# 128-row one-hot transposes and a re-ordered start in a routed-attention and MLP kernel

## Chip, cores, metric

One core of one Trainium2 chip. The metric is device time in microseconds (us) of one execution; the profile's "span" is some 1.9 us shorter than it. Engine names in the profile: PE is TensorE's matmuls, PEld its weight loads, DVE is VectorE, ACT ScalarE, POOL GpSimd, SP SyncE.

## The reference, cut to what matters

Four batches of eight heads, 768 rows of 64. A query attends only to keys whose nearest centroid (of 16 per head) is the same; then an MLP with exact GELU.

```python
q_assign = np.argmax(np.einsum('bhsd,hcd->bhsc', q_n, c_n), axis=-1)
k_assign = np.argmax(np.einsum('bhsd,hcd->bhsc', k_n, c_n), axis=-1)
mask = q_assign[:, :, :, None] == k_assign[:, :, None, :]
scores = scale * np.matmul(q, k.transpose(0, 1, 3, 2))
scores = np.where(mask, scores, -1000000000.0)
attn = np.exp(scores - max); attn = attn / attn.sum          # ... shortened
h = attn_out @ w_in;  out = gelu(h) @ w_out
```

## The kernel before

Each head goes through the same stations. GpSimd splits q and k into two fp16 parts (`split`: value and remainder). TensorE transposes them (`tr_pe`, six 128x128 blocks for q, six for k) into a tile in PSUM, the memory that TensorE writes its results to in this kernel (its parts are called banks), and VectorE copies that to `T`. TensorE multiplies `T` with the centroids (`asn`); VectorE sums two halves, takes the maximum, and compares (`onehot`). TensorE transposes the one-hots (`one_pe`) and VectorE writes them as 16 extra rows of `T`, scaled, so that the score matmul itself adds the mask. Six score pairs (`scores`) and six exps on ScalarE follow, then the product with v (`av`), its normalisation on VectorE (`norm`) and, every second head, a transpose of the output (`fin`). Heads 1 to 9 do their transposes on TensorE, as here; later heads use DMA transposes.

```python
ps_sc = ctx.enter_context(tc.tile_pool(name="ps_sc", bufs=2, space=PSUM))   # scores: 2 x 2 banks
ps_a = ctx.enter_context(tc.tile_pool(name="ps_a", bufs=1, space=PSUM))     # assignments: 1 bank
ps_x = ctx.enter_context(tc.tile_pool(name="ps_x", bufs=1, space=PSUM))     # output product: 1 bank
ps_o = ctx.enter_context(tc.tile_pool(name="ps_o", bufs=2, space=PSUM))     # all transposes: 2 banks
...
def one_pe(i):
    oh = ohs[(i // 2) % NOH]          # [128, N, 2 heads, q/k, 32]
    e = i % 2
    t_ps = ps_o.tile([128, S], FP16, tag="op", name="oh_ps")
    for j in range(N):
        nc.tensor.transpose(t_ps[0:64, j * 128:(j + 1) * 128],
                            oh[:, j, e].rearrange("p b c -> p (b c)"), ident)
    nc.vector.tensor_scalar(Ts[i][D:D + C, 1, :], t_ps[32:32 + C, :], -1.0, None, op0=ALU.add)
    nc.vector.tensor_scalar(Ts[i][D:D + C, 0, :], t_ps[0:C, :], float(VAL), None, op0=ALU.mult)
...
# the order of issue: g(i, c) is just after score pair c of head i
elif h < PT:                                          # heads 2 to 9
    o = 4 if h == 2 else 0
    at(g(0, 4) if h == 2 else g(h - 2, 0), tr_pe, h, 0)          # q
    at(g(0, 5) if h == 2 else g(h - 2, 2), tr_pe, h, 1)          # k
    at(g(1, 1) if h == 2 else g(h - 2, 4), prep_asn, h, h > 2)   # asn q, asn k, onehot
    at(g(h - 1, 1 + o // 2) if h < 11 else g(10, 4), one_pe, h)
```

In the traces below each engine's instructions come in the order of issue. The four pools take 4 + 1 + 1 + 2 = 8 PSUM banks.

The softmax here doesn't subtract the row's maximum and nothing guards it: scores larger than these inputs give would overflow.

Of the kernel before, what the change touches and what calls it, by code (L numbers as in the profile page):

```python
# [9 lines left out]
FP16 = mybir.dt.float16  # L10
# [10 lines left out]
def kernel(  # L21
# [10 lines left out]
    nc = tc.nc  # L32
# [3 lines left out]
    B, H, S, D = q.shape  # L36
    HC, C, _ = centroids.shape
    DM, DF = moe_w_in.shape
    N = S // 128
    NH = B * H  # L40
    QB = S // 2
# [17 lines left out]
    ps_sc = ctx.enter_context(tc.tile_pool(name="ps_sc", bufs=2, space=PSUM))  # L59
    ps_a = ctx.enter_context(tc.tile_pool(name="ps_a", bufs=1, space=PSUM))  # L60
    ps_x = ctx.enter_context(tc.tile_pool(name="ps_x", bufs=1, space=PSUM))
    ps_o = ctx.enter_context(tc.tile_pool(name="ps_o", bufs=2, space=PSUM))
# [3 lines left out]
    def load(i, keng=None, veng=None):  # L66
# [4 lines left out]
        for name, src, eng in (("q", q, nc.sync), ("k", k, keng or nc.sync),  # L71
# [9 lines left out]
    q_raw, k_raw, v_raw = [raw_pool.tile([128, N, D], FP32, tag=n + "_raw", name=n + "_raw")  # L81
                           for n in "qkv"]
# [13 lines left out]
    def warm(n, cols=512):  # L96
        for _ in range(n):
            nc.tensor.matmul(w_ps[:, 0:cols], ones[:, 0:128], ones[:, 0:cols],  # L98
                             start=True, stop=True)
# [3 lines left out]
    ident = const.tile([128, 128], FP16)  # L103
# [17 lines left out]
    NOH = 3  # L121
    ohs = [const.tile([128, N, 2, 2, 32], FP16, name=f"oh{t}") for t in range(NOH)]
    for t in ohs:
        nc.vector.memset(t[:, :, :, :, 16:32], 0.0)

    sts, vraws = {}, {}

# [17 lines left out]
    Ts = {}  # L145

    def tr_pe(i, w, copy=None, pool=None):
        if i not in Ts:
            Ts[i] = t_pool.tile([128, 2, S], FP16, tag="T", name="T")
        st = sts[i]  # L150
        pl, tag = pool or (ps_o, "op")
        t_ps = pl.tile([128, S], FP16, tag=tag, name="tr_ps")
        for j in range(N):
            nc.tensor.transpose(t_ps[:, j * 128:(j + 1) * 128], st[:, w, j, :], ident)  # L154
        (copy or nc.vector.tensor_copy)(Ts[i][:, w, :], t_ps)  # L155
# [17 lines left out]
    q1_raw, k1_raw, v1_raw = raws.pop(1)  # L173
    sts[1] = st_pool.tile([128, 2, N, 2 * D], FP16, tag="st", name="st")
    vraws[1] = v1_raw
    nc.gpsimd.tensor_tensor(cent_norm, cent_ssq, half, op=ALU.pow)
    nc.vector.tensor_sub(sts[0][:, 1, :, D:2 * D], k_raw, sts[0][:, 1, :, 0:D])

    tr_pe(0, 0, copy=nc.scalar.copy, pool=(ps_sc, "sc"))
    warm(1, 256)  # L180
# [10 lines left out]
    def cent_tr():  # L191
        chl_ps = ps_a.tile([128, 2, 128], FP16, tag="asn", name="chl_ps")
        for w in range(2):
            nc.tensor.transpose(chl_ps[:, w], cent_hl[:, w].rearrange("p a d -> p (a d)"),
                                ident)
        nc.vector.tensor_copy(c_all, chl_ps)

    def tr(i):
        st = sts.pop(i)
        Ts[i] = t_pool.tile([128, 2, S], FP16, tag="T", name="T")  # L200
        nc.sync.dma_start_transpose(
            out=Ts[i].rearrange("c w (n p) -> c (w n) p", p=128),
            in_=st.rearrange("p w n c -> p (w n c)"))
# [5 lines left out]
    def asn(i, which, halves=True):  # L209
        h = i % H  # L210
        chs = slice(h * C, (h + 1) * C)
        if which == 0:
            asns[i] = ps_a.tile([128, 512], FP32, tag="asn", name="asn_ps")
        a_ps = asns[i][:, 0:2 * NA].rearrange("p (n w l c) -> p n w l c", n=N, w=2, l=2)
        t = Ts[i][:, which]
        for j in range(N):
            js = slice(j * 128, (j + 1) * 128)
            if halves:
                nc.tensor.matmul(a_ps[:, j, which], t[:, js], c_all[:, :, chs],  # L219
                                 start=True, stop=True)  # L220
            else:
                for e in range(2):
                    nc.tensor.matmul(a_ps[:, j, which, 0], t[:, js], c_all[:, e, chs],  # L223
                                     start=(e == 0), stop=(e == 1))
# [35 lines left out]
    def one_pe(i):  # L260
        oh = ohs[(i // 2) % NOH]
        e = i % 2
        t_ps = ps_o.tile([128, S], FP16, tag="op", name="oh_ps")
        for j in range(N):
            nc.tensor.transpose(t_ps[0:64, j * 128:(j + 1) * 128],  # L265
                                oh[:, j, e].rearrange("p b c -> p (b c)"), ident)
        nc.vector.tensor_scalar(Ts[i][D:D + C, 1, :], t_ps[32:32 + C, :],  # L267
                                -1.0, None, op0=ALU.add)
        nc.vector.tensor_scalar(Ts[i][D:D + C, 0, :], t_ps[0:C, :],  # L269
                                float(VAL), None, op0=ALU.mult)  # L270

    def aug(i):
# [9 lines left out]
    def one_first():  # L282
        half_ps = []
        for e in range(2):
            t_ps = ps_o.tile([128, S], FP16, tag="op", name="oh_ps")
            for j in range(N // 2):
                nc.tensor.transpose(t_ps[0:64, j * 128:(j + 1) * 128],
                                    ohs[0][:, e * (N // 2) + j, 0].rearrange("p b c -> p (b c)"),
                                    ident)
            half_ps.append(t_ps)  # L290
        one_q, one_k = half_ps
        T0 = Ts[0][D:D + C]
        nc.scalar.activation(T0[:, 0, QB:S], one_k[0:C, 0:QB], ACT_FN.Copy, bias=0.0,
                             scale=float(VAL))
        nc.vector.tensor_scalar(T0[:, 0, 0:QB], one_q[0:C, 0:QB],
                                float(VAL), None, op0=ALU.mult)
        for o, z in ((0, 128), (128, QB)):
            nc.vector.tensor_scalar(T0[:, 1, o:z], one_q[32:32 + C, o:z],
                                    -1.0, None, op0=ALU.add)
        tr_pe(1, 1, pool=(ps_x, "x"))  # L300
        nc.vector.tensor_scalar(T0[:, 1, QB:S], one_k[32:32 + C, 0:QB],
                                -1.0, None, op0=ALU.add)

# [118 lines left out]
        nc.gpsimd.dma_start(out=w_chunks[n][0], in_=w_chunks[n][1])  # L422


    tr_pe(0, 1, copy=nc.scalar.copy, pool=(ps_sc, "sc"))
    warm(1)
    nc.scalar.copy(sts[1][:, 1, :, 0:D], k1_raw)
    nc.gpsimd.tensor_sub(sts[1][:, 1, :, D:2 * D], k1_raw, sts[1][:, 1, :, 0:D])
    cent_tr()
    nc.vector.tensor_sub(sts[1][:, 0, :, D:2 * D], q1_raw, sts[1][:, 0, :, 0:D])  # L430
    warm(2)
    asn(0, 0, halves=False)
    asn(0, 1, halves=False)
    onehot(0, halves=False)
    warm(1)
    tr_pe(1, 0, copy=nc.scalar.copy, pool=(ps_sc, "sc"))
    one_first()
    split(2, vnow=False)
    load_w(0)
# [44 lines left out]
    def at(t, fn, *args, **kw):  # L484
        events.append((t, len(events), fn, args, kw))

    T, TS = [], {}
    t = 0.0
    for i in range(NH + 1):
        for c in range(N):  # L490
            if (i, c) in FC1:
                b = FC1[i, c]
# [26 lines left out]
    def g(i, c):  # L519
        return TS[i, c] + 0.01  # L520
# [20 lines left out]
    for h in range(1, NH):  # L541
        pair = h - h % 2
        if h == 1:
            at(g(0, 0), asn, h, 0, False)
            at(g(0, 1), asn, h, 1, False)
            at(g(0, 1), onehot, h, False)
            at(g(0, 3), one_pe, h)
        elif h < PT:
            o = 4 if h == 2 else 0
            at(g(0, 4) if h == 2 else g(h - 2, 0), tr_pe, h, 0)  # L550
            at(g(0, 5) if h == 2 else g(h - 2, 2), tr_pe, h, 1)
            at(g(1, 1) if h == 2 else g(h - 2, 4), prep_asn, h, h > 2)
            at(g(h - 1, 1 + o // 2) if h < 11 else g(10, 4), one_pe, h)
        else:
            if pair < 10:
                at(g(pair - 2, 3) if h % 2 else g(pair - 3, 5), prep_asn, h)
                to, tg = T[pair] - g(pair - 2, 5), T[pair] - g(pair - 1, 2)
            else:
                ta, to, tg = (17.5, 12.0, 5.0) if pair >= 12 else (12.5, 7.0, 3.0)
                t0 = T[pair] - ta + 4.0 * (h % 2)  # L560
                at(t0, asn, h, 0)
                at(t0 + 1.2, asn, h, 1)
                at(t0 + 1.21, onehot, h)
            if h % 2 == 1:
                at(T[pair] - to, ohtr, pair)
                at(T[pair] - tg, aug, pair)
# [46 lines left out]
```

## Time and profile before

302.98 us (302.97 to 303.14, 3 runs). From the profile's page, busy times and the chain of work that ended last, by engine:

```profile
PE 296.4 (98%) x3109; PEld 186.0 (62%) x3109; DVE 121.7 (40%) x284; ACT 216.0 (72%) x274; POOL 106.8 (35%) x182
...
PE 97%; ACT 1%; DVE 1%; issue 0%; DVEq 0%
```

Both lines say TensorE. They are averages over stages, and one stage matters here: the attention of heads 0 to 9, before the first MLP.

| stretch of the trace | what the chain (where said, the timeline) shows |
|---|---|
| 0 to 9.35 us | loading, splitting, centroid chain, head 0's one-hot; first scores at 9.35 |
| 9.35 to 14.0 us | two exps (1.52 us), then head 1's one-hots on TensorE and VectorE; timeline: head 0's six exps back to back on ScalarE (4.48 us) |
| 14 to 47.6 us | TensorE in nearly every piece; 4.85 us a head |
| 47.6 to 55.5 us | two exps (1.63 us), then mostly TensorE; timeline: ScalarE's exps back to back (11 in 8.30 us) |
| from 55.5 us | MLP and later heads, TensorE |

The chain of one head in the third stretch (start, duration, what; x6 counts the instructions of a group):

```profile
25.29 0.45 PE oh_ps L265 x6
25.74 0.43 PE sc_ps L311 x2
26.17 0.18 PE x_ps L326 x6
26.35 0.33 PE tr_ps L154 x6
...
27.38 0.44 PE fin_ps L350 x6
...
28.33 0.29 PE asn_ps L219 x12
```

The one-hot group takes 0.45 us where the other six transposes (`tr_ps`) take 0.33.

The same head on VectorE in order of time (start, duration, engine, line, what; in brackets the idle time before it and what ended it):

```profile
23.61 0.56 DVE L232 TENSOR_REDUCE asum<-asn_ps 128x192 f32<-128x384 f32 x1 [0.41 <-PE asn_ps L219]
24.20 0.36 DVE L239 TENSOR_REDUCE asn_ps<-asum 128x12 f32<-128x192 f32 x1
24.59 0.35 DVE L240 TENSOR_TENSOR oh_167<-asum,asn_ps 128x192 f16<-128x192 f32 x1
24.87 0.19 DVE L336 RECIPROCAL rec<-x_ps 128x6 f32<-128x6 f32 x1
25.09 0.56 DVE L337 TENSOR_TENSOR x_tok<-x_ps,rec 128x384 f16<-128x384 f32 x1
25.56 0.55 DVE L155 COPY T<-tr_ps 128x768 f16<-128x768 f16 x1
26.14 0.55 DVE L267 TENSOR_SCALAR T<-oh_ps 16x768 f16<-16x768 f16 x1
26.71 0.55 DVE L269 TENSOR_SCALAR T<-oh_ps 16x768 f16<-16x768 f16 x1
27.29 0.56 DVE L155 COPY T<-tr_ps 128x768 f16<-128x768 f16 x1
27.86 0.56 DVE L352 COPY xt<-fin_ps 128x768 f16<-128x768 f16 x1
28.66 0.56 DVE L232 TENSOR_REDUCE asum<-asn_ps 128x192 f32<-128x384 f32 x1 [0.24 <-PE asn_ps L219]
```

From 20 us on VectorE has one wait a head, 0.41 or 0.24 us, always for the assignment matmuls, and is otherwise at work without a gap above 0.05 us.

### The profile page before, as it was taken

Reading aid. Unit: us, or ns where it says so; the run is one execution under the profiler, and the core shown is the slowest. Engines: PE = TensorE matmul, PEld = TensorE weight load, DVE = VectorE, ACT = ScalarE, POOL = GpSimd, SP = SyncE. Lnnn points to the kernel's source line nnn. Section 1 sums busy time; section 2 is a strip of 40 time slices with the busy share of each in tenths; the row PEclk is TensorE's granted clock in tenths of the full one; section 3 lists DMA queues with packets and bytes.
Section 4 is the critical chain, followed back from the end, with each engine's and each line's share of the span. In section 5 each row is a group of like instructions: output and inputs, shape, how many; then the busy total and the mean of one; then the engine's idle time right before and its main releaser. Section 6 shows DMA issues by size and latency. Waiting matters only on the chain.

```text
span 301.1 us, 7413 instructions
## 1 busy us (share of the span) xinstructions
PE 296.4 (98%) x3109; PEld 186.0 (62%) x3109; DVE 121.7 (40%) x284; ACT 216.0 (72%) x274; POOL 106.8 (35%) x182
## 2 busy tenths in 40 slices
PE   8899999999999999999999999999999999999996
PEld 4577777666666666666566666666566665565444
DVE  5788987103564742122353742213344413000112
ACT  5889999956888888856788888855788883466000
POOL 3999999997034104572633104600000000000000
PEclk9999999999999999999999999999999999999999
DMA  6999999994369348966679436876032242100122
GB/s 219 341 297 274 264 263 202 240 197 131 63 176 218 81 99 224 199 187 157 134 175 185 119 82 209 165 97 131 2 89 53 71 52 46 38 0 0 44 97 70
DMA packets 74065, 42.85 MB, mean 142 GB/s; under 512 B 54320, under 2 KB 71088, under 8 KB 74032
## 3 DMA queue, kind: packets, MB, share of 16 engines
q1 hardware_dynamic: 69520, 38.09, 53.4%
q0 software_dynamic: 4224, 4.19, 8.3%
q8 instruction: 24, 0.39, 0.5%
q10 hardware_dynamic: 288, 0.10, 0.1%
q14 instruction: 9, 0.07, 0.1%
HBM read 27.30 MB, written 6.29 MB: 112 GB/s over the span
## 4 chain that ended last, share of the span: by engine, by line
PE 97%; ACT 1%; DVE 1%; issue 0%; DVEq 0%
PE hp L386 27%; PE op L412 24%; PE sc_ps L311 21%; PE x_ps L326 11%; PE op_alt L412 3%; PE asn_ps L219 3%; PE tr_ps L154 2%; PE w_ps L98 1%; PE oh_ps L265 1%; ACT p_sb L314 1%; PE fin_ps L350 1%; PE asn_ps L223 0%; PE hp_early L367 0%; DVE T L269 0%; DVE T L267 0%
## 5 line engine op out<-in xcount | busy, mean ns | idle before, releaser
L314 ACT ACTIVATE p_sb<-sc_ps 128x768 f16<-128x768 f32 x192 | 149.7, 810 | 21.3 <-PE sc_ps L311 12.8
L311 PE MATMUL sc_ps<-T 80*128 80x384 f16 x384 | 93.8, 325 | 0.6 <-ACT p_sb L314 0.4
L386 PE MATMUL hp<-xt,w_in_sb 128*128 128x384 f16 x504 | 85.0, 326 | 0.0
L326 PEld LDWEIGHTS <-p_sb 128*128 128x128 f16 x1152 | 54.7, 97 | 30.8
L386 PEld LDWEIGHTS <-w_in_sb 128*128 128x128 f16 x504 | 47.9, 98 | 30.4
L132 POOL CAST st<-q_raw 128x384 f16<-128x384 f32 x30 | 15.4, 513 | 78.9 <-DMA q_raw<-in_q_dram 57.3
L416 DVE COPY o_sb<-op 128x512 f32<-128x512 f32 (+1 forms) x22 | 14.8, 672 | 55.0 <-PE op L412 54.9
L232 DVE TENSOR_REDUCE asum<-asn_ps 128x192 f32<-128x384 f32 x29 | 16.2, 558 | 50.8 <-PE asn_ps L219 50.7
L311 PEld LDWEIGHTS <-T 80*128 80x128 f16 x384 | 26.2, 97 | 5.8 <-issue 0.9
L133 POOL TENSOR_TENSOR st<-q_raw,st 128x384 f16<-128x384 f32 x30 | 27.3, 911 | 2.4
L135 POOL TENSOR_TENSOR st<-k_raw,st 128x384 f16<-128x384 f32 x30 | 27.4, 912 | 2.4
L336 DVE RECIPROCAL rec<-x_ps 128x6 f32<-128x6 f32 x32 | 6.2, 193 | 43.8 <-PE x_ps L326 43.8
L337 DVE TENSOR_TENSOR x_tok<-x_ps,rec 128x384 f16<-128x384 f32 x32 | 17.8, 558 | 1.1
L219 PEld LDWEIGHTS <-T 128*128 128x128 f16 x348 | 14.6, 96 | 4.4
L219 PE MATMUL asn_ps<-c_all,T 128*128 128x32 f16 x348 | 16.5, 177 | 0.0
L134 POOL CAST st<-k_raw 128x384 f16<-128x384 f32 x30 | 15.1, 505 | 0.0
L275 DVE TENSOR_SCALAR T<-ohT 16x768 f16<-16x768 f16 x22 | 7.9, 361 | 8.0 <-DMA ohT<-oh_166 3.6
L239 DVE TENSOR_REDUCE asn_ps<-asum 128x12 f32<-128x192 f32 x29 | 10.5, 361 | 1.0
L154 PE MATMUL tr_ps<-ident,st 128*128 128x128 f16 x120 | 10.6, 228 | 0.2 <-DVE T L269 0.2
L154 PEld LDWEIGHTS <-st 128*128 128x128 f16 x120 | 8.2, 101 | 2.9 <-DVE st L163 0.8
L155 DVE COPY T<-tr_ps 128x768 f16<-128x768 f16 x17 | 9.4, 554 | 0.6
L278 DVE TENSOR_SCALAR T<-ohT 16x768 f16<-16x768 f16 x22 | 8.6, 391 | 0.3
(308 smaller groups left out, 404.8 us busy)
## 6 DMA issues: line engine op xcount, KB each, us to landing
q_raw<-in_q_dram SPq DMA_DIRECT2D x32, 192.0 KB, 4.1
k_raw<-in_k_dram SPq DMA_DIRECT2D x32, 192.0 KB, 4.1
v_raw<-in_v_dram SPq DMA_DIRECT2D x32, 192.0 KB, 4.4
out_dram<-o_sb SPq DMA_DIRECT2D x23, 256.0 KB, 2.2
w_in_sb<-in_moe_w_in_dram POOLq DMA_DIRECT2D x4, 512.0 KB, 10.4
w_out_sb<-in_moe_w_out_dram POOLq DMA_DIRECT2D x4, 512.0 KB, 11.9
T<-st SPq DMA_TRANSPOSE x22, 4.9
xt<-x_tok SPq DMA_TRANSPOSE x11, 2.9
```

The costliest lines, as they stand in the source:

```text
L132: nc.gpsimd.tensor_copy(st[:, 0, :, 0:D], q_raw)
L133: nc.gpsimd.tensor_sub(st[:, 0, :, D:2 * D], q_raw, st[:, 0, :, 0:D])
L135: keng.tensor_sub(st[:, 1, :, D:2 * D], k_raw, st[:, 1, :, 0:D])
L154: nc.tensor.transpose(t_ps[:, j * 128:(j + 1) * 128], st[:, w, j, :], ident)
L219: nc.tensor.matmul(a_ps[:, j, which], t[:, js], c_all[:, :, chs], start=True, stop=True)
L232: nc.vector.tensor_reduce(out=asum, in_=a_ps.rearrange("p n w l c -> p n w c l"), axis=AX.X, op=ALU.add)
L311: nc.tensor.matmul(s_ps[:, t, 0:QB], Ts[i][0:D + C, 1, c * 128:(c + 1) * 128], Ts[i][0:D + C, 0, t * QB:(t + 1) * QB], start=True, stop=True)
L314: nc.scalar.activation(ps[i][:, c, :].rearrange("p (t q) -> p t q", t=2), s_ps[:, :, 0:QB], ACT_FN.Exp, bias=0.0, scale=float(scale))
L326: nc.tensor.matmul(x_ps[:, j], ps[i][:, ch, j * 128:(j + 1) * 128], va[:, ch, 0:D + 1], start=(ch == 0), stop=(ch == N - 1))
L337: nc.vector.tensor_tensor(xtoks[i - i % 2][:, :, i % 2, :], x_ps[:, :, 0:D], rec.to_broadcast([128, N, D]), op=ALU.mult)
L386: nc.tensor.matmul(hp[:, t, 0:QB], w_in_sb[:, m, f * 128:(f + 1) * 128], xts[b][:, m, t * QB:(t + 1) * QB], start=(m == 0), stop=(m == NM ...
L412: nc.tensor.matmul(op[:, 0:w], gs[b][f][:, js], w_out_sb[:, f, ms], start=(f == 0), stop=(f == NF - 1))
```

## The change

Its intent: one-hot transposes at the full 128 weight columns (both heads of a pair at once, half of it unused), and an earlier start: the remainder of head 0's keys goes from VectorE to GpSimd, head 0's transposed keys are copied in halves by two engines, the centroid chain comes sooner, head 1's steps are re-ordered around the one-hots, and head 2's first transposes come one slot sooner.

```diff
-        nc.vector.memset(t[:, :, :, :, 16:32], 0.0)
+        nc.vector.memset(t, 0.0)
...
-    nc.vector.tensor_sub(sts[0][:, 1, :, D:2 * D], k_raw, sts[0][:, 1, :, 0:D])
+    nc.gpsimd.tensor_sub(sts[0][:, 1, :, D:2 * D], k_raw, sts[0][:, 1, :, 0:D])
...
+    def tr_halves(i, w):       # three transposes each, copied by ScalarE and by VectorE
...
-            nc.tensor.transpose(t_ps[0:64, j * 128:(j + 1) * 128],
-                                oh[:, j, e].rearrange("p b c -> p (b c)"), ident)
-        nc.vector.tensor_scalar(Ts[i][D:D + C, 1, :], t_ps[32:32 + C, :],
+            nc.tensor.transpose(t_ps[:, j * 128:(j + 1) * 128],
+                                oh[:, j].rearrange("p a b c -> p (a b c)"), ident)
+        nc.vector.tensor_scalar(Ts[i][D:D + C, 1, :], t_ps[64 * e + 32:64 * e + 32 + C, :],
...                             # the same for q, and in head 0
-    tr_pe(0, 1, copy=nc.scalar.copy, pool=(ps_sc, "sc"))
     warm(1)
+    cent_tr()
+    tr_halves(0, 1)
...
-    cent_tr()
-    nc.vector.tensor_sub(sts[1][:, 0, :, D:2 * D], q1_raw, sts[1][:, 0, :, 0:D])
...                             # asn and onehot of head 0
-    tr_pe(1, 0, copy=nc.scalar.copy, pool=(ps_sc, "sc"))
+    nc.vector.tensor_sub(sts[1][:, 0, :, D:2 * D], q1_raw, sts[1][:, 0, :, 0:D])
...                             # inside one_first:
-        tr_pe(1, 1, pool=(ps_x, "x"))
+        tr_pe(1, 0, pool=(ps_x, "x"))
...                             # head 1 in the list of events
-            at(g(0, 0), asn, h, 0, False)
-            at(g(0, 1), asn, h, 1, False)
-            at(g(0, 1), onehot, h, False)
-            at(g(0, 3), one_pe, h)
+            at(g(0, 0), tr_pe, h, 1)
+            at(g(0, 1), asn, h, 0, False)
+            at(g(0, 2), asn, h, 1, False)
+            at(g(0, 2), onehot, h, False)
+            at(g(0, 4), one_pe, h)
...                             # heads 2 to 9
-            at(g(0, 4) if h == 2 else g(h - 2, 0), tr_pe, h, 0)
+            at(g(0, 3) if h == 2 else g(h - 2, 0), tr_pe, h, 0)
```

More of the change, by code (lines that the diff above doesn't have):

```diff
@@ L196, in cent_tr @@
         nc.vector.tensor_copy(c_all, chl_ps)
+    def tr_halves(i, w):
+        for e, (pl, tag, copy) in enumerate(((ps_sc, "sc", nc.scalar.copy),
+                                             (ps_o, "op", nc.vector.tensor_copy))):
+            t_ps = pl.tile([128, S], FP16, tag=tag, name="tr_ps")
+            for j in range(N // 2):
+                nc.tensor.transpose(t_ps[:, j * 128:(j + 1) * 128],
+                                    sts[i][:, w, e * (N // 2) + j, :], ident)
+            copy(Ts[i][:, w, e * QB:(e + 1) * QB], t_ps[:, 0:QB])
     def tr(i):
@@ L264, in one_pe @@
         for j in range(N):
-            nc.tensor.transpose(t_ps[0:64, j * 128:(j + 1) * 128],
-                                oh[:, j, e].rearrange("p b c -> p (b c)"), ident)
-        nc.vector.tensor_scalar(Ts[i][D:D + C, 1, :], t_ps[32:32 + C, :],
+            nc.tensor.transpose(t_ps[:, j * 128:(j + 1) * 128],
+                                oh[:, j].rearrange("p a b c -> p (a b c)"), ident)
+        nc.vector.tensor_scalar(Ts[i][D:D + C, 1, :], t_ps[64 * e + 32:64 * e + 32 + C, :],
                                 -1.0, None, op0=ALU.add)
-        nc.vector.tensor_scalar(Ts[i][D:D + C, 0, :], t_ps[0:C, :],
+        nc.vector.tensor_scalar(Ts[i][D:D + C, 0, :], t_ps[64 * e:64 * e + C, :],
                                 float(VAL), None, op0=ALU.mult)
@@ L286, in one_first @@
             for j in range(N // 2):
-                nc.tensor.transpose(t_ps[0:64, j * 128:(j + 1) * 128],
-                                    ohs[0][:, e * (N // 2) + j, 0].rearrange("p b c -> p (b c)"),
+                nc.tensor.transpose(t_ps[:, j * 128:(j + 1) * 128],
+                                    ohs[0][:, e * (N // 2) + j].rearrange("p a b c -> p (a b c)"),
                                     ident)
@@ L422, in load_w @@
         nc.gpsimd.dma_start(out=w_chunks[n][0], in_=w_chunks[n][1])
-    tr_pe(0, 1, copy=nc.scalar.copy, pool=(ps_sc, "sc"))
     warm(1)
+    cent_tr()
+    tr_halves(0, 1)
     nc.scalar.copy(sts[1][:, 1, :, 0:D], k1_raw)
     nc.gpsimd.tensor_sub(sts[1][:, 1, :, D:2 * D], k1_raw, sts[1][:, 1, :, 0:D])
-    cent_tr()
-    nc.vector.tensor_sub(sts[1][:, 0, :, D:2 * D], q1_raw, sts[1][:, 0, :, 0:D])
-    warm(2)
+    warm(1)
     asn(0, 0, halves=False)
@@ L434 @@
     onehot(0, halves=False)
-    warm(1)
-    tr_pe(1, 0, copy=nc.scalar.copy, pool=(ps_sc, "sc"))
+    nc.vector.tensor_sub(sts[1][:, 0, :, D:2 * D], q1_raw, sts[1][:, 0, :, 0:D])
+    warm(3)
     one_first()
```

## The prediction

> **What bounds the kernel now.** The page's busy shares: TensorE 98%, ScalarE 72%, VectorE 40%, GpSimd 35%; the chain that ended last is TensorE for 97%, at full clock. So there are two ways to gain: start the scores sooner, or take time off TensorE's queue. By the chain the first scores start at 9.35 us. Head 0 is then paced by ScalarE (six exps in 4.48 us, 0.75 each); from about 14 to 47.6 us TensorE paces (46 exps were done in 37.7 us, 0.82 apart); from 47.6 to 55.9 us ScalarE again (11 exps in 8.30 us). What follows is on TensorE and untouched by the change.
>
> **One-hot transposes (the larger part).** Heads 1 to 9 have a group of six with 64-column weights each, head 0 has one too. In the chain such a group takes 0.45 us, six 128-column transposes 0.34; the score pair right after it takes 0.43 us, other pairs 0.33. So the 64-column form costs about 0.21 us a head. The Trainium skill, "TensorE: Matmul & The Clock Gate", section on weight-path perf modes, says fast weight load is on only for 128 weights; "TensorEngine Tiling (Array Packing)", Key Properties, says that changing the tiling mode drains TensorE. Both fit, though no run shows the causes yet. Only groups in the TensorE-paced stretch count: heads 2 to 8, 7 x 0.21 = 1.5 us. Laying the chain's pieces with these cuts against exps 0.75 us apart and two score buffers gave an estimate of 1.5 us too. VectorE is busy 4.4 to 4.6 of 5 us there, and the period falls from 4.85 to about 4.65 us a head, so some is lost to its buffers: I count 1.35 us.
>
> **Start.** The key remainder leaves VectorE (0.56 us); on GpSimd it takes 0.91 us after the power (ends 4.65), so it ends near 5.55 against 4.88: worse. Bought back: the key copy, one ScalarE piece of 0.80 us ending near 6.75, becomes two halves side by side, ending near 6.65; the centroid transposes go first; so the assignment matmuls don't wait for keys and end near 7.15 instead of 7.40. Head 1's query remainder (0.56 us) now stands between the one-hot and its copies on VectorE, mostly behind the transposes, and gives back 0.1 us. First scores near 9.1: 0.2 to 0.25 us sooner.
>
> **Head 1.** One transpose group (0.34 us) moves from the idle wait before the scores into head 0's slots, where TensorE has slack (4.58 busy of 5). Its one-hot comes about 0.4 us later, but one VectorE copy goes ahead; its scores are ready (near 13.75) before ScalarE ends head 0 (near 14.1). Worth about 0; so are the larger memsets.
>
> **Sum.** 302.98 - 1.35 - 0.2 = 301.4 us, range 300.7 to 302.3. Faster by over 2%: 0.01; within 2%: 0.98; slower by over 2%: 0.01.
>
> **What would show each step.** One-hot groups in the chain at 0.34 us and the scores after them at 0.33; head periods near 4.65 us in 20 to 47 us; first scores at about 9.1 us; the first MLP stage (55.5 us before) about 1.5 us earlier, and the rest as long as before.
>
> **What would make it wrong.** The 0.10 us after a one-hot group belongs to something else, halving the gain; ScalarE or VectorE soaks it up (TensorE waits for exps or for a freed PSUM buffer); GpSimd's key remainder is slowed by VectorE beside it, or head 1's later one-hot opens a gap near 13 us: then 302.3 or more. If heads 1 and 9 count too: 300.9.

## The result, and the profile after

The changed kernel takes 303.1 us (302.97 to 303.27, 4 runs), the kernel before 303.0 (302.97 to 303.14, 4 runs). The ratio is 1.0003, 95% interval 0.9985 to 1.002: the same, where 1.6 us less had been expected. Here and below, a ratio is the mean time of one kernel's fast runs over that of the other's in the same rounds, so it is not quite the ratio of the medians quoted.

The page of the changed kernel, busy times and chain by engine:

```profile
PE 296.0 (98%) x3110; PEld 186.6 (62%) x3110; DVE 123.0 (41%) x285; ACT 214.1 (71%) x273; POOL 108.0 (36%) x183
...
PE 94%; DVE 2%; ACT 2%; DMA 1%; issue 0%
```

The chain of the same head (line numbers are 9 higher than before):

```profile
25.39 0.34 PE oh_ps L274 x6
25.72 0.42 PE sc_ps L320 x2
26.14 0.18 PE x_ps L335 x6
26.32 0.44 PE tr_ps L154 x6
...
27.45 0.47 PE fin_ps L359 x6
...
28.44 0.29 PE asn_ps L228 x12
```

The one-hot group did fall from 0.45 to 0.34 us, as predicted. But the next transpose group rose from 0.33 to 0.44, and `fin_ps` from 0.44 to 0.47: what TensorE saved it spent a microsecond later, waiting. The score pair after the one-hots hardly moved (0.42 against 0.43). VectorE tells what TensorE waited for (in brackets the idle time before an instruction and what ended it):

```profile
25.66 0.55 DVE L155 COPY T<-tr_ps 128x768 f16<-128x768 f16 x1
26.24 0.55 DVE L276 TENSOR_SCALAR T<-oh_ps 16x768 f16<-16x768 f16 x1
26.81 0.55 DVE L278 TENSOR_SCALAR T<-oh_ps 16x768 f16<-16x768 f16 x1
27.39 0.56 DVE L155 COPY T<-tr_ps 128x768 f16<-128x768 f16 x1
27.96 0.56 DVE L361 COPY xt<-fin_ps 128x768 f16<-128x768 f16 x1
28.77 0.56 DVE L241 TENSOR_REDUCE asum<-asn_ps 128x192 f32<-128x384 f32 x1 [0.24 <-PE asn_ps L228]
```

Each line lies 0.10 or 0.11 us behind its partner of before, and the idle time is the same 0.24: VectorE keeps its pace to the hundredth, only shifted. The first copy ends at 26.21, which frees one of the two PSUM buffers for transposes; TensorE's second transposes, which by the order of allocation take that buffer, start at 26.27 in its timeline. At 17.88 to 21.56 us the chain of the changed kernel itself runs on VectorE, through the one-hot copies, the sum and the comparison to that first copy, and from there to the second transposes (21.60, 0.49 us). From VectorE's reciprocals, head for head, the period is 4.86 us (24.97 to 44.41 over four heads) against 4.85 before (24.87 to 44.27).

The start did not come sooner either: first scores at 9.33 us against 9.35. And head 1's first scores came later, 14.20 against 14.01:

```profile
13.59 0.56 DVE L278 TENSOR_SCALAR T<-oh_ps 16x768 f16<-16x768 f16 x1
...
14.20 0.11 PEld L320 LDWEIGHTS <-T 80*128 80x128 f16 x2 [0.71 <-DVE T L278]
```

The weight load of those scores waits for VectorE's one-hot copy of head 1 and starts 0.05 us after it ends (14.15). The profile puts the matmul's own wait down to ScalarE, whose last exp of head 0 ends at 14.20 too; with two score buffers that matmul needs only an earlier exp. ScalarE had run out of scores by then (its first exp of head 1 shows 0.54 us of idle time before it, 0.18 before the change).

Theories put to the test ("paces" means: sets the time of one head). **V**: in the stretch of 17 to 47 us a loop paces: VectorE's instructions of a head in a row, and one trip through TensorE (transposes into the freed buffer, assignment matmuls) back to VectorE's next sum. A TensorE saving outside that trip becomes a wait. **T**: TensorE paces after all, and the 128-column form only moved its cost to the next group. **S**: ScalarE's exps pace. (GpSimd, busy 4.75 to 4.83 of 5 us there, is no further candidate: it works ahead at 4.12 us a head, 24.09 to 28.21, the profile shows no engine waiting for it in 18 to 45 us, and a_hi below gets to 4.655 us a head with its work untouched.) **L**, for the start: VectorE's centroid scaling is held up by GpSimd's key remainder.

### The profile page after: what moved, and what is told of

Same layout as the page of the kernel before. It is cut to its first block, busy times and chain, and to the rows that moved or that the text cites. A ratio compares the mean times of both kernels' runs of the same rounds, so it can differ in the third digit from the quotient of the medians.

```text
span 301.2 us, 7415 instructions
## 1 busy us (share of the span) xinstructions
PE 296.0 (98%) x3110; PEld 186.6 (62%) x3110; DVE 123.0 (41%) x285; ACT 214.1 (71%) x273; POOL 108.0 (36%) x183
## 4 chain that ended last, share of the span: by engine, by line
PE 94%; DVE 2%; ACT 2%; DMA 1%; issue 0%
PE hp L395 27%; PE op L421 24%; PE sc_ps L320 20%; PE x_ps L335 11%; PE op_alt L421 3%; PE asn_ps L228 3%; ACT p_sb L323 2%; PE tr_ps L154 2%; DMA q_raw<-in_q_dram 1%; PE oh_ps L274 1%; PE fin_ps L359 1%; PE asn_ps L232 0%; PE hp_early L376 0%; PE w_ps L98 0%; DVE asum L241 0%
## 5 line engine op out<-in xcount | busy, mean ns | idle before, releaser
L154 PE MATMUL tr_ps<-ident,st 128*128 128x128 f16 x114 | 9.8, 223 | 0.2
```

The costliest lines, as they stand in the source:

```text
L154: nc.tensor.transpose(t_ps[:, j * 128:(j + 1) * 128], st[:, w, j, :], ident)
```

## The experiments

All kernels gave correct results in the comparison, the two with a reduced assignment too. "Before" is the kernel before, run on the same chip in the same rounds.

| run | what | us | before | ratio (95%) |
|---|---|---|---|---|
| b_oh128 | before + 128-row one-hots | 302.89 | 303.00 | 0.9996 (0.9982 to 1.001) |
| a_hi | changed, VectorE's sum cut | 301.65 | 303.00 | 0.9954 (0.9941 to 0.9968) |
| b_hi | before, VectorE's sum cut | 302.24 | 303.00 | 0.9976 (0.9964 to 0.9989) |
| a_re | changed, one-hots later | 305.44 | 303.00 | 1.0078 (1.0065 to 1.0092) |
| a_split | changed, assignment split | 302.65 | 303.21 | 0.9984 (0.9972 to 0.9996) |
| b_split | before, assignment split | 302.74 | 303.21 | 0.9987 (0.9975 to 0.9999) |
| b128_split | before + 128-row + split | 302.28 | 303.21 | 0.9973 (0.9961 to 0.9985) |
| a_cact | changed, scaling on ScalarE | 303.11 | 303.21 | 0.9997 (0.9985 to 1.0008) |
| b128_psa | b128_split + other bank | 303.17 | 302.96 | 1.0004 (0.9992 to 1.0016) |
| b_psa | b_split + other bank | 303.28 | 302.96 | 1.0010 (0.9998 to 1.0022) |
| a_psa | a_split + other bank | 303.71 | 302.96 | 1.0030 (1.0016 to 1.0044) |
| a_kdve | changed, key remainder on VectorE | 303.06 | 302.96 | 1.0006 (0.9994 to 1.0018) |
| a_h1 | a_split, head 1 as before | 302.60 | 302.92 | 0.9989 (0.9977 to 1.0002) |
| b128_s2 | b128_split, first copy sooner | 303.45 | 302.92 | 1.0017 (1.0004 to 1.0031) |

### The one-hots alone: b_oh128

```diff
 # kernel before, with the change's edits to memset, one_pe and one_first only
```

> The kernel before with the 128-row one-hot transposes alone. Theory V (VectorE's loop paces the stretch 17 to 47 us: its 14 to 15 instructions a head back to back, plus one wait for the assignment matmuls): within 0.3 us of 303.0, one-hot groups at 0.34 us in the chain, the transposes and assignment groups after them longer by as much. My prediction's account (TensorE paces): 1.35 us faster, 301.6.

302.89 us, 0.1 below before, inside V's 0.3 and far from my 301.6. Its profiled execution took 605 us, with a granted clock of 0.979 (a slower state that some executions fall into), and is not used, so what V expected of its groups was not checked on it; b128_split below has the same one-hots in a fast one. So the miss is not a gain lost to the other parts of the change: the one-hots alone are worth next to nothing.

### Taking work off VectorE: a_hi and b_hi

A result wrong on purpose: heads 3 to 9 are assigned by the high half of the centroids alone, so that VectorE's sum of the two halves (0.56 us) goes, while TensorE issues as many matmuls as before (each with 16 moving columns, not 32).

```diff
-                for e in range(2):
+                ne = 1 if i in HI else 2           # HI = range(3, 10)
+                for e in range(ne):
                     nc.tensor.matmul(a_ps[:, j, which, 0], t[:, js], c_all[:, e, chs],
-                                     start=(e == 0), stop=(e == 1))
+                                     start=(e == 0), stop=(e == ne - 1))
...
-            ... prep_asn, h, h > 2)
+            ... prep_asn, h, h > 2 and h not in HI)
```

> The changed kernel, wrong result on purpose: heads 3 to 9 are assigned by the high half of the centroids alone, so VectorE loses the 0.56 us sum of each of 7 heads, while TensorE issues as many assignment matmuls as before. Theory V: VectorE's loop falls from 4.86 to about 4.3 us a head, ScalarE (4.5) or TensorE (4.5 to 4.65) paces next, so 1.5 to 2.5 us faster than 303.1. Rival T (TensorE paces, the saving of the one-hots was given back on TensorE itself, for instance in the pair after them): within 0.3 us of 303.1. Rival S (ScalarE paces): within 0.3 us too.

> The same cut of VectorE's sum on the kernel before. Theory V: faster than 303.0, but by less than on the changed kernel, since the 64-column one-hots then cost TensorE 0.11 to 0.21 us a head for 7 heads: 0.8 to 1.5 us slower than a_hi. Rivals T and S: within 0.3 us of 303.0.

a_hi is 1.35 us below before on its chip, b_hi 0.76. T and S fall: no matmul and no exp was taken away, and the narrower assignment matmuls gave TensorE little (0.28 us in place of 0.29 for the twelve where neither waits). a_hi stays a little short of the 1.5 us that V named (against the changed kernel's 303.1 us of other rounds it is 1.45), and the two lie 0.6 us apart, less than the 0.8 named: a_hi has the changed start, and its head 1 began 0.45 us later than b_hi's (14.41 against 13.96). The chain of a_hi, then of b_hi, in the same head:

```profile
25.05 0.34 PE oh_ps L276 x6
25.39 0.42 PE sc_ps L322 x2
25.81 0.18 PE x_ps L337 x6
25.99 0.34 PE tr_ps L154 x6
...
27.02 0.34 PE fin_ps L361 x6
```

```profile
24.95 0.45 PE oh_ps L267 x6
25.40 0.43 PE sc_ps L313 x2
25.83 0.18 PE x_ps L328 x6
26.01 0.34 PE tr_ps L154 x6
...
27.04 0.34 PE fin_ps L352 x6
```

With VectorE's load cut, every group of six 128-column transposes takes 0.34 us, `fin_ps` too: the 0.44 and 0.47 of the two original kernels were 0.34 of work and a wait. Now TensorE paces (its transpose and assignment groups all take the shortest time that any run shows for them), and its own period can be read: 4.655 us a head in a_hi (24.07 to 42.69 over four heads), 4.785 in b_hi (23.96 to 43.10). That is the true worth of the wide form where TensorE paces: 0.13 us a head, 0.11 in the group and 0.02 in the pair after it. And the kernel before, at 4.85, was only 0.065 above TensorE's own 4.785: TensorE looked like the pace-maker because it nearly was.

### Filling VectorE's wait by order: a_re

```diff
-            at(g(h - 1, 1 + o // 2) if h < 11 else g(10, 4), one_pe, h)
+            at(g(h - 1, 3 if h < 9 else 1), one_pe, h)
```

> The changed kernel with correct result; one line: the one-hot transposes of heads 3 to 8 come two slots later, behind the second transposes of the head after, so that VectorE has the two one-hot copies to do while it now waits for the assignment matmuls. No instruction is added or removed. Theory V: the wait of 0.41 and 0.24 us a head closes over 6 heads, 1.5 to 2 us faster than 303.1. Rivals T and S: within 0.3 us, or slower.

2.4 us slower than before: V's expectation failed. The period rose to 5.26 us (25.81 to 46.84). VectorE's timeline with the later one-hots:

```profile
27.38 0.56 DVE L155 COPY T<-tr_ps 128x768 f16<-128x768 f16 x1 [0.32 <-PE tr_ps L154]
28.40 0.55 DVE L276 TENSOR_SCALAR T<-oh_ps 16x768 f16<-16x768 f16 x1 [0.47 <-PE oh_ps L274]
```

VectorE now waits 0.79 us in this head, since the things it does next come from TensorE later, and TensorE in turn waits for the normalised output (its weight loads for the output product show 0.43 us of idle time before them). So the pace is not set by the sum of VectorE's work alone, but by how the two queues hand over to each other; my first form of V was too simple.

### Shortening the trip through TensorE: a_split, b_split, b128_split

The query half of the assignment matmuls comes one slot sooner; nothing is added.

```diff
-            at(g(1, 1) if h == 2 else g(h - 2, 4), prep_asn, h, h > 2)
+            if h == 2:
+                at(g(1, 1), prep_asn, h, False)
+            else:
+                at(g(h - 2, 3), asn, h, 0)
+                at(g(h - 2, 4), asn, h, 1)
+                at(g(h - 2, 4), onehot, h)
```

> The changed kernel, result correct; for heads 3 to 9 the query half of the assignment matmuls comes one slot sooner, so that only the key half (6 matmuls, about 0.18 us, not 12 in 0.36) stands between VectorE's last transpose copy and its next sum. No instruction is added. Theory V (a loop: VectorE's work of a head in a row, then one trip through TensorE's assignment matmuls): VectorE's wait of 0.41 us falls to about 0.25, the head period from 4.86 to about 4.7 us, 0.7 to 1.2 us faster than 303.1. If VectorE's or TensorE's plain throughput paces, and not the loop: within 0.3 us.

> The same on the kernel before (64-column one-hots). Theory V with the period that TensorE alone showed in b_hi (4.77 us a head, against 4.65 in a_hi): 0.3 to 0.8 us faster than 303.0, TensorE then pacing at about 4.77.

> The kernel before with the 128-row one-hots and the split assignment, with the start of before. Theory V: faster than b_split by 0.3 to 0.8 us (7 heads at 0.12 less what is left of the loop), and equal to or faster than a_split by up to 0.3, as head 1's scores come sooner in the order of before. If the one-hot width is worth nothing even where TensorE paces: equal to b_split.

Period 4.79 us in a_split (24.88 to 44.05), 4.81 in b_split (24.82 to 44.07), 4.79 in b128_split (24.53 to 43.69). VectorE's 0.24 us wait in the heads with an output transpose went, and the 0.41 in the other heads stayed, where half of it was expected to go: there TensorE arrives late at the key half, having waited for the freed buffer (0.49 us for the second transposes in the chain of a_split). a_split gained 0.56 us on before, less than the 0.7 named; b_split gained 0.47, as expected. b128_split gained 0.93: 0.46 more than b_split, inside the 0.3 to 0.8 named, and 0.37 more than a_split, a little over the 0.3 named. But the 0.46 came only in part as expected, from 0.12 us a head: the periods differ by 0.02, and of the lead in the profiled executions 0.29 was there at the second reciprocal already (24.53 against 24.82), 0.08 of it from loads that came sooner and 0.10 from head 1. To that extent the number was right by luck. **b128_split is the best correct version: 302.28 us, below the kernel before in the same rounds, and below the changed kernel's 303.1 of other rounds**, with one schedule edit and the 128-row form, without the new start.

### Another bank for the one-hots: b128_psa, b_psa, a_psa

```diff
-        t_ps = ps_o.tile([128, S], FP16, tag="op", name="oh_ps")
+        pl, tag = (ps_a, "asn") if 3 <= i <= 8 else (ps_o, "op")
+        t_ps = pl.tile([128, S], FP16, tag=tag, name="oh_ps")
```

> b128_split, result correct, with the one-hot transposes of heads 3 to 8 written to the PSUM bank of the assignments, which is free then, so that a head's second transpose group finds the other transpose buffer free. Theory V, sharpened (the loop runs VectorE's work, then its first transpose copy, which frees one of two PSUM buffers, then TensorE's second transposes up to the assignment matmuls, 4.66 us in heads without the output transpose): the second transposes wait no longer (0.34 us in place of 0.44 to 0.49), the period falls from 4.79 towards TensorE's own 4.65 us, 0.5 to 1.0 us faster than b128_split: 301.3 to 301.8. If the buffer is not on the loop: within 0.2 us of b128_split.

> The same with the 64-column one-hots. With the buffer out of the way TensorE paces, at about 4.77 us a head: 302.3 to 302.7. The difference to b128_psa is what the one-hot width is worth once TensorE paces: 0.7 to 1.1 us (0.12 us for heads 2 to 8, and 0.2 at head 1). Rival: the width is worth nothing, equal to b128_psa.

> The same two schedule edits on the changed kernel: as b128_psa in the stretch, but 0.2 to 0.5 us slower in all, for the start of the change and its order of head 1 (first scores of head 1 at 14.1 to 14.2 against 13.8).

By the ratios, all three came out slower than their partners without the bank edit: b_psa by 0.7 us, b128_psa by 0.9 (where 0.5 to 1.0 faster was expected), a_psa by 1.4. b_psa missed its 302.3 to 302.7, and a_psa lies 0.5 above b128_psa, at the edge of the 0.2 to 0.5 named. From the chain of b128_psa:

```profile
22.00 0.57 DVE T L270
22.56 0.05 issue
22.61 0.32 PE asn_ps L219 x6
...
26.27 0.34 PE tr_ps L154 x6
```

Half of the expectation held: the second transposes wait no longer (0.34 us), so it was the buffer that they had waited for. But the query half of the assignments now waits for the same bank until VectorE has copied the one-hots out (ends 22.56, matmuls from 22.61): the wait moved one group on, and grew. The period is 4.895 us (24.88 to 44.46). The two widths differ by 0.1 us here, not by 0.7 to 1.1: TensorE doesn't pace here either.

### First copy sooner: b128_s2

```diff
-            at(g(0, 4) if h == 2 else g(h - 2, 0), tr_pe, h, 0)
+            at(g(0, 4) if h == 2 else g(h - 2, 0) if h in (3, 9) else g(h - 3, 4) + 0.02, tr_pe, h, 0)
```

> b128_split, result correct, with the first transposes of heads 4 to 8 emitted two slots sooner, so that VectorE copies them (and frees their buffer) before the normalisation of the head and not behind it. Theory V (the buffer freed by the first copy starts TensorE's half of the loop): the second transposes wait no longer, the period falls from 4.79 by up to 0.13, 0.2 to 0.8 us faster than b128_split, 301.5 to 302.1. It may fail if the normalised output now comes too late for the next product (a wait before the output products of 0.2 us or more): then equal or slower.

0.5 us slower than before, and by the ratios 1.3 slower than b128_split, where 0.2 to 0.8 faster was expected. Again the named wait went (second transposes at 0.34 us), and again the time came back elsewhere: the transposes now stand before a score pair and ScalarE's exps enter the chain (0.82 us of one exp in each head). The expectation allowed for a failure by another route, a wait before the output products of 0.2 us or more: at 21.3 us that is there (0.54 us, 0.24 in b128_split at the same place), in the next head it is 0.17.

### The start: a_cact and a_kdve

a_cact scales the centroids on ScalarE, ahead of its first transpose copy; a_kdve puts the key remainder back on VectorE.

```diff
 # a_cact (the two VectorE steps before it move up with it)
-    nc.vector.tensor_scalar_mul(cent_hl[:, 0], cent_sb.unsqueeze(1).to_broadcast(...), cent_rnorm)
+    nc.scalar.mul(cent_hl[:, 0], cent_sb.unsqueeze(1).to_broadcast(...), cent_rnorm)
 # a_kdve
-    nc.gpsimd.tensor_sub(sts[0][:, 1, :, D:2 * D], k_raw, sts[0][:, 1, :, 0:D])
+    nc.vector.tensor_sub(sts[0][:, 1, :, D:2 * D], k_raw, sts[0][:, 1, :, 0:D])
```

> The changed kernel, result correct, with the centroid scaling moved from VectorE to ScalarE. Theory L (at the start, VectorE's scaling waits for GpSimd's key remainder beside it: 0.54 to 0.75 us in place of 0.29, ending 0.08 us after it, each time): the scaling takes 0.3 us and the first scores come 5.3 to 5.45 us after the centroid power starts, in place of 5.62 to 5.74, so 0.2 to 0.3 us faster than 303.1. Rival (the start is bound by the key remainder and its two copies alone): first scores and time unchanged.

> The changed kernel with the key remainder of head 0 back on VectorE, at its place before the centroid chain; all else as changed. Theory L: with nothing large on GpSimd beside it the centroid scaling takes 0.29 us again; it starts behind the remainder, so the first scores come 5.2 to 5.5 us after the centroid power starts, against 5.62 to 5.74, and 0.1 to 0.3 us faster than the changed kernel, if centroids land as early. Rival: the scaling stays at 0.54 to 0.82 us, so GpSimd's remainder was not its cause.

What L rests on, first in the changed kernel, then in the kernel before:

```profile
4.47 0.91 POOL L177 TENSOR_TENSOR st<-k_raw,st 128x384 f16<-128x384 f32 x1 [0.20 <-ACT st L172]
4.72 0.74 DVE L183 TENSOR_SCALAR cent_hl<-cent_sb,cent_rnorm 128x128 f16<-128x128 f32 x1
```

```profile
5.18 0.29 DVE L183 TENSOR_SCALAR cent_hl<-cent_sb,cent_rnorm 128x128 f16<-128x128 f32 x1
```

The same instruction takes 0.29 us before and 0.74 after, and ends (5.46) 0.08 us after GpSimd's subtraction (5.38). In a_hi, a_re, a_psa, a_split and a_h1, all with the changed start, it took 0.54, 0.54, 0.54, 0.82 and 0.84 us, and each time it ended 0.08 us after GpSimd's. a_kdve, with nothing large on GpSimd, has 0.29 again, and a_cact 0.40 on ScalarE. So the stall is real, 0.25 to 0.55 us, and GpSimd's instruction is its cause. The Trainium skill, "SBUF — State Buffer", section "Who interferes with whom", states the rule: VectorE in a mode with two ports and GpSimd take a shared pair of ports for a whole instruction, and the later one blocks. These numbers agree with it; that this instruction ran in such a mode is not in the trace.

But lifting the stall did not shorten the time. a_cact's first scores come 5.46 us after the centroid power starts, just outside the 5.3 to 5.45 named and below the 5.61 to 5.74 of the five kernels with the changed start as it is; its time is 303.11 us, 0.1 below before, where 0.2 to 0.3 had been named. In a_kdve they come 5.86 us after it, and the time is 303.06, 0.1 above before: a miss, the remainder on VectorE now stands ahead of the centroid chain itself. The times of arrival of the first loads blur this: the first VectorE instruction, which waits for q, started between 3.20 and 3.48 us from run to run, whatever the kernel. Measured from there, the first scores came after 5.93 to 6.09 us in the seven traces with the start of before and after 5.86 to 6.36 in the five with the changed start and order (before, b_hi, b_split, b128_split, b128_psa, b_psa, b128_s2; after, a_hi, a_re, a_split, a_psa). No start was shown to be faster.

Sorted by the arrival of the centroids, the traces say a little more. Where the centroid power started 0.17 to 0.24 us after that first VectorE instruction, the first scores came after 5.93 to 6.04 us with the start of before (b_hi, b_split, b128_split, b128_psa, b128_s2) and after 5.86 and 5.94 with the changed one (after, a_split). Where it started 0.61 to 0.65 us after, they came after 5.98 and 6.09 (b_psa, before) and after 6.22 to 6.36 (a_hi, a_re, a_psa). So in these traces the changed start gains next to nothing when the centroids come early, and loses 0.1 to 0.4 us when they come late. a_cact, a late one, has 6.08: with the stall lifted its first scores came 0.14 to 0.28 us sooner than theirs.

### Head 1's order: a_h1

```diff
 # a_split, with head 1's steps as in the kernel before:
+    tr_pe(1, 0, copy=nc.scalar.copy, pool=(ps_sc, "sc"))      # before head 0's one-hots
-            at(g(0, 0), tr_pe, h, 1)                           # and the events of before
 ...
```

> a_split with the start of the change (key remainder on GpSimd, key copy in halves, centroid transposes first) but head 1 in the order of before. If the order of head 1 is what costs: head 1's first scores come 4.55 to 4.6 us after head 0's, as in before, b_split and b128_split (4.57 to 4.67), not 4.85 to 4.87 as in every kernel with the change's order, and the time is 0.2 to 0.4 us below a_split, 302.25 to 302.5. If the start costs: equal to a_split, 302.65, with that gap still closed.

The gap between head 0's and head 1's first scores is 4.57 us, as with the old order; every kernel with the new order shows 4.86 or 4.87 (after, a_hi, a_re, a_split, a_cact, a_psa, a_kdve). So the new order costs 0.3 us there (a_h1 puts head 2's first transposes back as well, so the two are not told apart). The time, 302.60 us, is only 0.05 below a_split and misses the 302.25 to 302.5 named: in its trace the first scores came at 9.41 us against a_split's 9.25 (q arrived within 0.02 us of it), so there the old order gave back at the start half of what it gained at head 1, and what is left is below what these runs resolve.

## Why the prediction was wrong

- **Wrong step: "from about 14 to 47.6 us TensorE paces".** From it followed "Only groups in the TensorE-paced stretch count: heads 2 to 8, 7 x 0.21 = 1.5 us". The runs show a loop of VectorE and TensorE at 4.85 us a head in that stretch, with TensorE's own work at 4.785 (b_hi) and 4.655 (a_hi). Shortening TensorE from the one to the other left the period at 4.86; the 4.65 that I had named came only with VectorE's sum gone. The gain became waits. The largest is for a transpose buffer that VectorE frees (0.33 to 0.44 us in the next transposes; gone in b128_psa, where that buffer is free). Together they make up the whole difference: a_hi's 4.655, and in the changed kernel 0.10 more in `tr_ps` of each head, 0.13 more in `fin_ps` of every second head (0.47 against 0.34) and 0.08 more in `asn_ps` of the other heads (0.37 against 0.29) give 4.86.
- **How it came about.** I read the chain's TensorE pieces as work. Some held waits of 0.1 us: with matmul records of 219 ns and only 56 ns between starts (0.34 us for six), neighbouring records overlap and such a wait leaves no idle time in the page, which showed TensorE busy for 5.00 of 5 us. The Trainium skill, "Perfetto Trace Analysis", section "Per-instruction lifecycle: what the profiler-reported window actually captures", says that a matmul's end is estimated and not observed; such overlapping records fit that, though no run here shows the true ends. `fin_ps` at 0.44 us next to 0.33 for the same six transposes was the clue.
- **The size of the one-hots, 0.21 us a head, was 0.13** where TensorE paces. The group's 0.11 was right. The other 0.10, the pair after the group, was listed under "what would make it wrong" and did belong to something else: the pair takes 0.41 to 0.42 us with the 128-column form too, so a drain on the way back to 128 columns is at most some 0.02 us of it. What the rest is stays open.
- **"Some is lost to its buffers: I count 1.35 us"**, 0.15 taken off 1.5, named the right suspect and gave it a tenth of its weight.
- **The start, 0.2 us: not reached.** The predicted GpSimd time of 0.91 us was right, and it "is slowed by VectorE beside it" was named as a risk; it was the reverse, VectorE held up by GpSimd, 0.25 to 0.55 us of the centroid chain. That this is where the gain went is in part argued: in the traces with late centroids a_cact's first scores came 0.14 to 0.28 us sooner than with the stall, but its time did not come down, and the loads' arrival varies by 0.3 us.
- **Head 1, "Worth about 0", cost 0.3 us** (4.87 against 4.57 between first scores). Its one-hot came 0.8 us later (12.34 against 11.55), not 0.4, and its last copy ended at 14.15, not near 13.75. In the kernel before, head 1's wide one-hots were worth 0.1 us (4.67 to 4.57).
- **Right:** the direction of each single piece on TensorE, and that little of the time lies outside the stretch: the rest of the kernel, from the first MLP on, took as long as before (from the table load for the first GELU to the end, 55.97 to 301.2 us against 55.91 to 301.1).

## What to carry to other kernels

Before costing a saving on the engine that the chain names, look at the second engine of the stretch in order of time, not by its busy share: if it runs without a gap but for one wait that comes back each round, suspect a loop of the two and test it by taking work off the second one. If it is a loop, the saving is worth only what the first engine's own work exceeds the loop by (here nothing: 4.785 us of work in a loop of 4.85). Two groups of the same instructions with different durations in the chain (0.33 and 0.44 us) mean that one of them holds a wait. And of four re-orderings here one gained (the split), two took away the wait that they aimed at and lost more at the next hand-over (the other bank, the sooner copy), and one made the wait longer (a_re): in this kernel cutting work (a_hi, 1.35 us, though with a wrong assignment) was surer than moving it.

## What the Trainium skill lacked or had wrong

- "TensorEngine Tiling (Array Packing)", Key Properties: it says that a change of tiling mode drains TensorE, with no cost. Here the step from 64-column weights back to 128 cost no more than 0.02 us a group (pair after it 0.43 against 0.41 to 0.42 us). That this step is a change of mode is my reading of the profile's 128\*64 beside the 128\*128 of the neighbours; a cost on the way in would be within the group's 0.11 us.
- "TensorE: Matmul & The Clock Gate", the section on weight-path perf modes: it gives about 2x for fast weight load. That agrees: the weight loads' records here show 110 ns for 64 columns and 97 for 128, 1.72 against 0.76 ns a column; a group of six transposes takes 0.45 against 0.34 us. The formula of the same page's section on LDWEIGHTS, columns over 1.2, gives an estimate of 53 ns for a 64-column load, where the record has 110; the six, with their matmuls, take 75 ns each from start to start.
- "SBUF — State Buffer", "Who interferes with whom": the rule held. It has no time for a small VectorE instruction: 0.29 us became 0.54 to 0.84 us beside a 0.91 us GpSimd subtraction, and ended 0.08 us after it.
- "Perfetto Trace Analysis": it says that matmul busy time misleads, but not that a wait of 0.1 us leaves no idle time at all: TensorE was shown busy for 5.00 of 5 us (25 to 30 us) while it waited about 0.1 us at one group of a head.
